# A third store behind k's blocks, sums of x in other pairs, a first pair's weight behind its total

## The chip, the cores and the metric

The program runs on one core of a Trainium2 chip. The metric is the device time of one execution in microseconds (us); the time before is the median of three runs. A profiled execution of its own, with a span from its first to its last instruction, gives all durations below.

## The reference

Attention in which a query sees only the keys that fall into its hash bucket, and a two-layer network behind it:

```python
q_bits = (np.einsum('bhsd,dk->bhsk', q, proj) > 0)      # 6 bits of each query, k likewise
mask = q_bucket[:, :, :, None] == k_bucket[:, :, None, :]
scores = np.where(mask, scale * q @ k.T, -1e9)
x = softmax(scores) @ v            # (4, 8, 768, 64) -> (3072, 512)
h = x @ w_in                       # (512, 2048)
g = np.maximum(h, 0.0) + alpha * np.minimum(h, 0.0)
out = g @ w_out                    # (2048, 512)
```

There are 4 batches of 8 heads, 768 positions each, 64 numbers a head. The weights come as 64-bit floats and are rounded to 32-bit ones on the chip.

## The kernel before

The work has two parts. The first runs over 16 pairs of heads (`pi` from 0 to 15, four pairs a batch). The second runs over blocks of the two matrix products, each built from seven smaller products in place of eight, which is why sums and differences of quarters of x, w_in, g and w_out are formed; `sum_x` forms those of x, and `sums_due` holds those of w_in.

In a pair, TensorE makes twelve cells of scores (L786: two matmuls on the hash bits `qb` and `kb`, four on q and k), ScalarE takes the exponential of each into `pt` (L789), then TensorE makes the next pair's hash bits (L738), multiplies the probabilities with v (`av`, L819, 96 matmuls), and sums columns for the softmax (`sm`, L832, in `totals`), which needs VectorE's total `accd` of the six blocks of probabilities. VectorE forms that total in five additions of 1.75 us each (`add_first` L797, `add_third` L805, `add_last` L801 and L802, `add_total` L808). The scores use a ring of three PSUM buffers (`two_banks`), which `sm`, the hash products and the turned alpha (L561) share.

The next pair's iteration opens with `divide` of the pair before: VectorE turns the sums (L846) and takes reciprocals, GpSimd copies four small blocks (L855, L856), VectorE spreads them (L858) and scales (L864). The result goes to DRAM as `x_s` (L865), from which `load_x` (L879) gets the quarters of batch 0 later. Between these lies `weight_begin`: the turn of the next pair's k blocks (L718), work on a weight piece, in four of the pairs a `sum_x` (L889), and the pair's first addition.

Each pair also rounds two weight pieces: `weight_abs` (ScalarE L606, L610, or VectorE L608), `weight_clamp` (L616), `weight_parts` (L622), `weight_sum` (L647, L650). Four pieces of w_in make a group; four sums on GpSimd (L669) follow, at most two a pair, and then the group's store: four DMAs (L674) into `w_in_s`, 448 KB each. There are four groups, so four stores. `load_w` (L895) later reads 896 KB of `w_in_s` for one block of the second part.

The order of work is the order of the program for everything inside `do(...)`; `pinned(when, ins)` does so only if `when` is true. DMAs outside are placed by the scheduler. One queue, SP's, issues almost all loads and stores, one after the other: at the end of pair `pi` those of v for pair `pi + 2` (L491), stores that are due, `load_w`, `load_x`, and the q and k blocks of pair `pi + 3` (L517, four DMAs each). Those blocks are turned by VectorE (L718) at the end of pair `pi + 1` (q) and at the start of pair `pi + 2` (k). The hash bits are moved into `qb` and `kb` by small DMAs on ScalarE's and GpSimd's queues (L747). GpSimd also issues the loads of the weight pieces (L592).

Of the kernel before, what the change touches and what calls it, by code (L numbers as in the profile page):

```python
# [407 lines left out]
def fast_path(  # L408
# [12 lines left out]
    nc = tc.nc  # L421
# [21 lines left out]
    do = tc.keep_in_program_order  # L443
# [66 lines left out]
    def load_blocks(pi, name):  # L510
        b, hp = pairs[pi]
        src = {"q": q, "k": k}[name]
        nat[name, pi] = t = pool.tile([P, NC * 4, 32], F32, name=f"{name}n{pi}", tag=f"{name}n", bufs=3)
        for s in range(2):
            for h in range(2):
                a = D * s + 32 * h
                nc.sync.dma_start(  # L517
                    t[a : a + 32].rearrange("i (c u) d -> i c u d", u=4),
                    src[b, 2 * hp + s, :, 32 * h : 32 * h + 32].rearrange("(u i c) d -> i c u d", u=4, c=NC),
                )  # L520

    nil = []

# [64 lines left out]
    def load_weight(i, queue=nc.gpsimd):  # L588
        if i < NW:
            i = order[i]  # L590
            raw[i] = pool.tile([P, 512], moe_w_in.dtype, name=f"raw{i}", tag="raw", bufs=3)
            queue.dma_start(raw[i], piece(i))  # L592
# [8 lines left out]
    def weight_abs(i, engine=None):  # L601
        i = order[i]
        lo, hi = halves(i)
        wx[i] = pool.tile([P, 512], F32, name=f"wx{i}", tag="wx")
        wr[i] = pool.tile([P, 512], I32, name=f"wr{i}", tag="wr")
        do(ACT.activation(wr[i], lo, AF.Copy, scale=2.0 ** -29))  # L606
        if engine is DVE:
            do(DVE.tensor_scalar(wx[i].bitcast(U32), hi, 0x7FFFFFFF, None, op0=ALU.bitwise_and))  # L608
            return
        do(ACT.activation(wx[i], hi.bitcast(F32), AF.Abs))  # L610

    def weight_clamp(i):
        if i < NW:
            i = order[i]
            x = wx[i]
            do(DVE.tensor_scalar(x, x, HI_MIN, None, op0=ALU.max, op1=ALU.max, accum_out=wmax[:, i : i + 1]))  # L616

    def weight_parts(i):
        i = order[i]
        x = wx[i].bitcast(U32)  # L620
        turned = i < HW and i % 4 == 3
        do(DVE.tensor_scalar(  # L622
            x, x, 3, 0x40000000 if turned else 0xC0000000, op0=ALU.logical_shift_left, op1=ALU.bitwise_xor,
        ))

    def weight_sum(i):


        i = order[i]
        lo, hi = halves(i)  # L630
        x = wx[i]
        if i < HW:
            n, m = divmod(i, 4)
            if m == 0:
                wst[n] = pool.tile([P, NM, 4, P], F32, name=f"wsi{n}", tag="wsi")
            slot = (0, 5, 1, 2)[m]
            dst = wst[n][:, slot].rearrange("p i f -> p (i f)")
        else:
            n, m = divmod(i - HW, 2)
            if m == 0:  # L640
                wst[HW + n] = pool.tile([P, 4, DM // 2], F32, name=f"wso{n}", tag="wso")
            w = wst[HW + n]
            dst = w[:, 0:4:3] if m == 0 else w[:, 1:3]
        x, r = x.bitcast(I32), wr[i]
        if i >= HW:
            hi, x, r = (t.rearrange("p (a f) -> p a f", a=2) for t in (hi, x, r))
        do(DVE.scalar_tensor_tensor(  # L647
            x.bitcast(U32), hi, 0x80000000, x.bitcast(U32), op0=ALU.bitwise_and, op1=ALU.bitwise_xor,
        ))
        do(DVE.tensor_tensor(dst.bitcast(I32), x, r, op=ALU.add))  # L650
        return (dst if i < HW else dst[:, 0])[:, :1]
# [3 lines left out]
    def weight_group(i):  # L655

        i = order[i]
        if i >= HW:
            n, m = divmod(i - HW, 2)
            if m == 1:  # L660
                nc.sync.dma_start(w_out_r[:, :, n].rearrange("m p d -> p m d"), wst[HW + n])
            return
        n, m = divmod(i, 4)
        if m < 3:
            return
        w = wst[n]

        def one(to, a, op, c):
            do(POOL.tensor_tensor(w[:, to], w[:, a], w[:, c], op=op))  # L669

        def store():
            c, kk = divmod(n, 2)
            for ii in range(4):
                do(nc.sync.dma_start(w_in_s[4 * c + ii][:, :, kk], w[:, :, ii]))  # L674


        for x in ((3, 5, 2), (5, 0, 5), (4, 3, 0), (6, 1, 4)):
            sums_due.append((one, (x[0], x[1], ALU.subtract, x[2])))
        sums_due.append((stores_due.append, (store,)))
# [5 lines left out]
    def weight_sums(count, after=None):  # L685

        if sums_due and after is not None:
            do(POOL.tensor_copy(late_sum, after))
        while sums_due and (count or sums_due[0][0].__name__ != "one"):
            fn, x = sums_due.pop(0)  # L690
            count -= fn.__name__ == "one"
            fn(*x)
            if now_stored and stores_due:
                stores_due.pop()()
# [21 lines left out]
    def turn_blocks(pi, name):  # L716
        tr[name, pi] = pool.tile([P, S], F32, name=f"{name}T{pi}", tag=f"{name}T")
        do(DVE.transpose(tr[name, pi], nat[name, pi].rearrange("p w d -> p (w d)")))  # L718
# [88 lines left out]
    def add_total(pi):  # L807
        do(DVE.tensor_tensor(accd[pi], accd[pi], accp[pi], op=ALU.add))  # L808
# [61 lines left out]
    def pinned(when, ins):  # L870

        if when:
            do(ins)
# [10 lines left out]
    def sum_x(b, n, engine):  # L884

        to, a, c = ((3, 5, 0), (5, 2, 5), (4, 2, 3), (6, 4, 1))[n]
        if to != 5:
            x_m[b, to] = mid.tile([P, 2, CW], F32, name=f"x{b}_{to}", tag=f"x{to}", bufs=1)
        do(engine.tensor_tensor(x_m[b, to], x_m[b, a], x_m[b, c], op=ALU.subtract))  # L889

    def load_w(n):

        if n < B * NI:
            w_m[n] = mid.tile([P, NM, 2, P], F32, name=f"wi{n}", tag="wi", bufs=3)
            pinned(n < 3, nc.sync.dma_start(w_m[n], w_in_s[n % NI]))  # L895
# [297 lines left out]

    for pi in range(NPAIR):
        i = 2 * pi
        if pi == 14:
            now_stored.append(pi)

        def weight_begin():
            if pi == 1:  # L1200
                turn_blocks(2, "q")
            if pi + 1 < NPAIR:
                turn_blocks(pi + 1, "k")
            weight_clamp(i)
            weight_parts(i)
            if pi in (8, 10, 12, 14):
                sum_x(0, (8, 10, 12, 14).index(pi), DVE)
            add_first(pi)

        if pi == 1:  # L1210
            scores(1, CELLS[:3])
            weight_abs(3)
            scores(1, CELLS[3:])
            divide(0, weight_begin)
        elif pi:
            scores(pi, CELLS)
            divide(pi - 1, weight_begin)
        else:
            rest = [c for c in CELLS if c not in ahead]
            scores(pi, rest[:4])  # L1220
            weight_abs(0, DVE)
            scores(pi, rest[4:])
            add_first(pi)
            weight_clamp(0)
            weight_parts(0)
        weight_sum(i)
        weight_group(i)
        load_weight(i + 3)
        if pi == 0:
            weight_abs(1, DVE)  # L1230
        weight_clamp(i + 1)
        add_third(pi)
        add_last(pi)
        add_total(pi)
        weight_parts(i + 1)
        weight_sums(1, weight_sum(i + 1))
        weight_group(i + 1)
        load_weight(i + 4)
        if pi + 1 < NPAIR:
            hash_bits(pi + 1)  # L1240
            do(ACT.activation(tr["q", pi + 1], tr["q", pi + 1], AF.Copy, scale=DOWN))  # L1241
        if 0 < pi < NPAIR - 2:
            turn_blocks(pi + 2, "q")
        attend(pi)
        if pi + 1 == NPAIR:
            now = ff1(0, 0)
            now.step(1)
        totals(pi)
        if pi + 1 == NPAIR:
            now.step(5)  # L1250
            divide(pi)
        else:
            weight_abs(i + 2)
        if pi + 2 < NPAIR:
            load(pi + 2, "v")
        while stores_due and pi < 14:
            stores_due.pop(0)()
        if pi in (9, 11, 15):
            load_w((9, 11, 15).index(pi))
        if pi in (4, 5, 7, 8):  # L1260
            load_x(0, {4: 0, 5: 3, 7: 2, 8: 1}[pi])
        if pi == 1:
            setup_alpha()
        for name in "qk":
            magnitude(pi, name)
            if pi + 3 < NPAIR:
                load(pi + 3, name)
        if 0 < pi < NPAIR - 1:
            weight_abs(i + 3)

# [96 lines left out]
```

## Time and profile before

| what | value |
|---|---|
| median of three runs | 874.98 us (873.43 to 875.38) |
| profiled execution, its own time | 872.97 us |
| its span | 871.19 us |
| TensorE's mean granted clock | 0.997 |
| bytes moved by DMA | 135.36 MB, 155 GB/s on average |

| `sm` (L832) of pair | starts at, us | since the one before |
|---|---|---|
| 0 | 28.65 | |
| 1 | 48.15 | 19.50 |
| 2 | 67.59 | 19.44 |
| 3 | 86.57 | 18.98 |
| 8 | 181.47 | 18.98 |
| 9 | 200.50 | 19.03 |
| 12 | 257.44 | 18.98 |
| 13 | 278.13 | 20.69 |
| 14 | 297.78 | 19.65 |
| 15 | 318.03 | 20.25 |

The second table is read from the timeline of TensorE: as every pair has one such group of matmuls, at the same place in its work, the distance between two of them is the time of a pair. A line of a timeline has the start and the duration in us, the engine, the line of the program, the operation, the tile that it writes and those that it reads, and in brackets how long the engine was idle before it and what ended that. SPq is SP's queue; a row there is the issue of DMAs, not their transfer. `x3` means three instructions in a row.

### The profile page before, as it was taken

To read this page: it belongs to the slowest core of one execution; us is meant where nothing else is said; L and a number is where in the kernel's file an instruction comes from. 1 tells how busy PE (TensorE), PEld (TensorE's weight loads), DVE (VectorE), ACT (ScalarE), POOL (GpSimd) and SP (SyncE) were. 2 spreads that over 40 slices of the span, in tenths; PEclk is the share of its full clock that TensorE was granted. 3 is DMA by queue.
4 is the path that set the end of the run, shared out by engine and by line. 5 is a ranking of instruction groups with operands and counts; after the bars stand their busy time and mean duration, and the time that the engine had idled before them with its cause. 6 is when DMAs were issued, how large, how long until landed. Compare 5 with 4: busy or idle time off the path is not lost.

```text
span 871.2 us, 14629 instructions
## 1 busy us (share of the span) xinstructions
PE 859.3 (99%) x5458; PEld 574.3 (66%) x5458; DVE 733.7 (84%) x1188; ACT 375.2 (43%) x682; POOL 121.5 (14%) x249
## 2 busy tenths in 40 slices
PE   9999999999999999999999999999999999999996
PEld 4444444444444445569995559996558997557996
DVE  6999999999998987899897669897659898568886
ACT  6687888878777733331113331112332112232111
POOL 1322423434424410210000000000000000000001
PEclk9999999999999999999999999999999999999998
DMA  8855779789696446785334344433425334420242
GB/s 196 178 146 130 176 180 248 176 215 232 130 265 158 148 131 237 262 288 221 118 116 121 133 134 156 123 145 90 175 86 170 138 109 127 151 84 1 97 163 61
DMA packets 171105, 135.36 MB, mean 155 GB/s; under 512 B 126240, under 2 KB 155088, under 8 KB 167440
## 3 DMA queue, kind: packets, MB, share of 16 engines
q1 hardware_dynamic: 158528, 108.44, 43.6%
q0 software_dynamic: 9488, 24.56, 9.2%
q10 hardware_dynamic: 3008, 1.33, 0.6%
q8 instruction: 45, 0.74, 0.4%
q14 instruction: 36, 0.29, 0.1%
HBM read 104.87 MB, written 28.31 MB: 153 GB/s over the span
## 4 chain that ended last, share of the span: by engine, by line


## 5 line engine op out<-in xcount | busy, mean ns | idle before, releaser
L786 PE MATMUL sc<-qT,kT 64*128 64x384 f32 x768 | 155.4, 482 | 0.0
L789 ACT ACTIVATE pt<-sc 128x768 f32<-128x768 f32 x192 | 151.8, 812 | 4.7 <-PE sc L786 4.5
L819 PE MATMUL av<-pt,vn 128*32 128x385 f32 (+1 forms) x1536 | 127.0, 485 | 0.0
L819 PEld LDWEIGHTS av<-pt,vn 128*32 128x32 f32 x1536 | 50.3, 109 | 73.8 <-issue 70.2
L786 PEld LDWEIGHTS sc<-qT,kT 64*128 64x128 f32 x768 | 68.9, 187 | 34.8 <-issue 34.0
L979 DVE TENSOR_TENSOR g<-g,g 128x384 f32<-128x384 f32 x128 | 68.4, 555 | 2.2
L1098 POOL DMA_DIRECT2D out_dram<-o x4 | 2.2, 555 | 472.8 <-DVE o L1091 472.8
L786 PE MATMUL sc<-qb,kb 64*128 64x384 bf16 x384 | 64.2, 324 | 1.5 <-DVE st L846 0.9
L975 DVE SCALAR_TENSOR_TENSOR g<-h,alpha 128x384 f32<-128x384 f32 x60 | 36.9, 614 | 25.2 <-ACT h L968 25.1
L1036 DVE TENSOR_TENSOR ws<-wl 128x512 f32<-128x512 f32 x56 | 38.5, 687 | 20.6 <-DMA wl<-w_out_s 18.8
L1044 DVE TENSOR_TENSOR gs<-g,gs 128x768 f32<-128x768 f32 x56 | 53.3, 952 | 1.0
L1044 DVE TENSOR_TENSOR gs<-g 128x768 f32<-128x768 f32 x56 | 53.3, 952 | 0.0
L786 PEld LDWEIGHTS <-kb 64*128 64x128 bf16 x384 | 21.3, 94 | 37.5 <-issue 13.7
L606 ACT ACTIVATE wr<-raw 128x512 int32<-128x512 uint32 x32 | 22.1, 691 | 33.4 <-DVE wso L650 17.8
L797 DVE TENSOR_TENSOR accp<-pt,pt 128x1536 f32<-128x1536 f32 x16 | 28.1, 1756 | 6.1 <-ACT pt L789 6.1
L747 POOL DMA_DIRECT2D qb<-hr x60 | 30.0, 507 | 21.3 <-ACT hr L742 21.3
L802 DVE TENSOR_TENSOR accd<-accd,pt 128x1536 f32<-128x1536 f32 x16 | 28.1, 1759 | 1.7
L808 DVE TENSOR_TENSOR accd<-accd,accp 128x1536 f32<-128x1536 f32 x16 | 28.1, 1758 | 0.6
L805 DVE TENSOR_TENSOR accp<-accp,pt 128x1536 f32<-128x1536 f32 x16 | 28.1, 1754 | 0.0
L801 DVE TENSOR_TENSOR accd<-pt,pt 128x1536 f32<-128x1536 f32 x16 | 28.0, 1752 | 0.0
L1241 ACT ACTIVATE qT<-qT 128x768 f32<-128x768 f32 x15 | 12.7, 845 | 26.7 <-DMA kb<-hr 16.2
L919 PE MATMUL f_0a<-x,wi 128*128 128x384 f32 x64 | 23.5, 490 | 0.0
(366 smaller groups left out, 1768.4 us busy)
## 6 DMA issues: line engine op xcount, KB each, us to landing
wi<-w_in_s SPq DMA_DIRECT2D x32, 896.0 KB
wl<-w_out_s SPq DMA_DIRECT2D x16, 1024.0 KB
wl<-w_out_r SPq DMA_DIRECT2D x12, 1024.0 KB
raw<-in_moe_w_in_dram POOLq DMA_DIRECT2D x15, 512.0 KB, 5.3
raw<-in_moe_w_out_dram POOLq DMA_DIRECT2D x14, 512.0 KB, 4.8
w_in_s<-wsi SPq DMA_DIRECT2D x16, 448.0 KB
qn<-in_q_dram SPq DMA_DIRECT2D x64, 96.0 KB
vn<-in_v_dram SPq DMA_DIRECT2D x16, 384.0 KB
```

Of the source, the lines that this page charges most:

```text
L747: queue.dma_start(bits[name, pi][D * s : D * s + 2 * NB, half * CW : (half + 1) * CW], raw[c : c + 2 * NB],)
L786: do(PE.matmul(sc[:, s, :CW], what["k", pi][r, ks], what["q", pi][r, qs], start=first, stop=not first,))
L789: do(ACT.activation(pts[kc][:, g, :, :CW], sc[:, :, :CW], AF.Exp, scale=SCALE / DOWN))
L797: do(DVE.tensor_tensor(accp[pi], p(0), p(1), op=ALU.add))
L802: do(DVE.tensor_tensor(accd[pi], accd[pi], p(5), op=ALU.add))
L805: do(DVE.tensor_tensor(accp[pi], accp[pi], p(2), op=ALU.add))
L808: do(DVE.tensor_tensor(accd[pi], accd[pi], accp[pi], op=ALU.add))
L819: do(PE.matmul(av[pi][D * s + t : D * s + t + 32, g, :w], nat["v", pi][:, s, kc * D + t : kc * D + t + 32], pts[kc][:, g, s, :w], start=(k ...
L975: do(DVE.scalar_tensor_tensor(new_g(b, m)[:, i], h, al, h, op0=ALU.mult, op1=ALU.max))
L979: do(DVE.tensor_tensor(new_g(b, to)[:, i], g_m[b, x][:, i], g_m[b, y][:, i], op=ALU.subtract))
L1036: do(DVE.tensor_tensor(t, w2[b, n, x], w2[b, n, y], op=op))
L1044: do(DVE.tensor_tensor(t, g2[b, n, x], g2[b, n, y], op=ALU.subtract))
```

## The change

Six things change in the order of the program; no operation is added or removed.

1. In pair 0, the second weight piece (L608, L616) follows the pair's total instead of standing ahead of `add_third`. Its `weight_sum` and the load of the next piece move further, into `divide` of pair 0 in the iteration of pair 1, ahead of the turn of q's blocks.
2. The third store of w_in's sums (group 2) is issued in pair 11 behind the loads of q and k, whose blocks for pair 14 are pinned in program order (k alone needs it). In the other pairs the loop that issues due stores is as it was.
3. The second `load_w` moves from pair 11 to pair 12.
4. The sums of x move from pairs 8, 10, 12, 14 to 6, 9, 12, 15.
5. The loads of x move from pairs 4, 5, 7, 8 to 3, 4, 6, 9.
6. The fourth store is no longer pinned, and `now_stored` is set from pair 12 on; on SP the store keeps its place.

```diff
-                nc.sync.dma_start(
+                pinned(name == "k" and pi == 14, nc.sync.dma_start(
                     t[a : a + 32].rearrange("i (c u) d -> i c u d", u=4),
...
-                do(nc.sync.dma_start(w_in_s[4 * c + ii][:, :, kk], w[:, :, ii]))
+                pinned(n < 3, nc.sync.dma_start(w_in_s[4 * c + ii][:, :, kk], w[:, :, ii]))
...
-        if pi == 14:
+        if pi == 12:
             now_stored.append(pi)
+
+        def weight_end(i):
+            weight_sums(1, weight_sum(i))
+            weight_group(i)
+            load_weight(i + 3)
 
         def weight_begin():
             if pi == 1:
+                weight_end(1)
                 turn_blocks(2, "q")
...
-            if pi in (8, 10, 12, 14):
-                sum_x(0, (8, 10, 12, 14).index(pi), DVE)
+            if pi in (6, 9, 12, 15):
+                sum_x(0, (6, 9, 12, 15).index(pi), DVE)
             add_first(pi)
...
-        if pi == 0:
-            weight_abs(1, DVE)
-        weight_clamp(i + 1)
+        if pi:
+            weight_clamp(i + 1)
         add_third(pi)
         add_last(pi)
         add_total(pi)
+        if pi == 0:
+            weight_abs(1, DVE)
+            weight_clamp(1)
         weight_parts(i + 1)
-        weight_sums(1, weight_sum(i + 1))
-        weight_group(i + 1)
-        load_weight(i + 4)
+        if pi:
+            weight_end(i + 1)
...
-        while stores_due and pi < 14:
+        while stores_due and pi < 10:
             stores_due.pop(0)()
-        if pi in (9, 11, 15):
-            load_w((9, 11, 15).index(pi))
-        if pi in (4, 5, 7, 8):
-            load_x(0, {4: 0, 5: 3, 7: 2, 8: 1}[pi])
+        if pi in (9, 12, 15):
+            load_w((9, 12, 15).index(pi))
+        if pi in (3, 4, 6, 9):
+            load_x(0, {3: 0, 4: 3, 6: 2, 9: 1}[pi])
...
+        if stores_due and pi == 11:
+            stores_due.pop()()
```

More of the change, by code (lines that the diff above doesn't have):

```diff
@@ L516, in load_blocks @@
                 a = D * s + 32 * h
-                nc.sync.dma_start(
+                pinned(name == "k" and pi == 14, nc.sync.dma_start(
                     t[a : a + 32].rearrange("i (c u) d -> i c u d", u=4),
                     src[b, 2 * hp + s, :, 32 * h : 32 * h + 32].rearrange("(u i c) d -> i c u d", u=4, c=NC),
-                )
+                ))
     nil = []
```

## The prediction

> **What bounds the kernel now.** First the page's busy times, then its row of 40 slices:
>
> ```profile
> PE 859.3 (99%) x5458; PEld 574.3 (66%) x5458; DVE 733.7 (84%) x1188; ACT 375.2 (43%) x682; POOL 121.5 (14%) x249
> ...
> PE   9999999999999999999999999999999999999996
> ```
>
> TensorE is busy for 859.3 of 871.2 us and its clock is full, so only its 11.9 us of gaps can be won or widened. The table of windows of 20 us says where they lie:
>
> ```profile
> 20.00:40.00 20.00, 18.70 (x180) 8.95 (x176) 18.96 (x27) 14.39 (x24) 5.36 (x13) 1.00 0.95 163
> ...
> 240.00:260.00 20.00, 19.93 (x192) 9.67 (x189) 18.80 (x26) 15.71 (x25) 5.83 (x13) 1.00 1.00 270
> 260.00:280.00 20.00, 19.05 (x186) 8.91 (x183) 17.51 (x25) 13.81 (x21) 6.37 (x15) 1.00 0.67 162
> 280.00:300.00 20.00, 19.53 (x190) 9.49 (x188) 19.27 (x27) 15.28 (x24) 9.95 (x17) 1.00 0.39 123
> ```
>
> (Columns: window, length, PE, PEld, DVE, ACT, POOL, clock, DMA share, GB/s.) From 320 us on every window but the last has PE at 19.99 or 20.00; the tail is not touched. So I read the attention part by its clock: the sums matmuls `sm` (L832), one group a pair. On the PE timeline they start at 28.65, 48.15, 67.59, 86.57, 105.55 and so on, 18.98 apart, until 257.44; then 278.13, 297.78, 318.03. Periods above 18.98 are lost time: 0.52 (pair 1), 0.46 (pair 2), 1.71 (13), 0.67 (14); pair 15 has other work in it (20.25). What ended the gaps, from the timelines of PE, weight loads, VectorE and the SP queue:
>
> ```profile
> 28.65 0.85 PE L832 MATMUL sm<-accd,ones 128*32 128x384 f32 x8 [0.97 <-DVE accd L808]
> ...
> 258.20 0.09 PEld L786 LDWEIGHTS <-kb 64*128 64x128 bf16 x1 [0.62 <-DMA kb<-hr]
> ...
> 260.81 0.34 PE L786 MATMUL sc<-qb,kb 64*128 64x384 bf16 x2 [0.41 <-DVE st L846]
> ...
> 278.13 0.85 PE L832 MATMUL sm<-accd,ones 128*32 128x384 f32 x8 [0.54 <-DVE accd L808]
> ```
>
> ```profile
> 259.31 0.98 DVE L718 STREAM_TRANSPOSE qT<-qn 128x768 f32<-128x768 f32 x1 [0.82 <-DMA qn<-in_q_dram]
> ...
> 263.44 0.98 DVE L718 STREAM_TRANSPOSE kT<-kn 128x768 f32<-128x768 f32 x1 [2.11 <-DMA kn<-in_k_dram]
> ```
>
> ```profile
> 242.29 5.81 SPq L674 DMA_DIRECT2D w_in_s<-wsi  x4
> 248.15 0.70 SPq L895 DMA_DIRECT2D wi<-w_in_s  x1
> 248.89 1.86 SPq L517 DMA_DIRECT2D qn<-in_q_dram  x2
> 250.85 8.29 SPq L517 DMA_DIRECT2D kn<-in_k_dram  x4
> ```
>
> The third store and a `wi` load stand ahead of pair 14's q and k blocks on SP. The blocks come late, VectorE stands still 0.82 + 2.11 us (it has about 0.7 us to spare a pair: its usual wait at L797), and TensorE waits for it in pairs 13 and 14.
>
> **What the Trainium skill says.** "DMA: Bandwidth & Descriptors", Queues, rings and completion order: each DMA engine consumes a queue's descriptors in ring order. The trace agrees: q's blocks, issued by 250.75, were waited for until 259.31, behind 1.79 MB of store and 0.90 MB of `wi` (2.69 MB at the 341 to 365 GB/s of 244 to 252 us is an estimated 7.6 us). Same page, Issuing engines are not separate DMA queues: DMAs of SP, ScalarE and GpSimd share the same 16 engines. Agrees: the hash bits `qb`, on GpSimd's queue, took 6.6 us to land between 245 and 265 against a median of 4.1. "SBUF — State Buffer", SBUF: two separate sides: a VectorE operation with two SBUF inputs and a GpSimd operation that reads SBUF exclude each other. Agrees: GpSimd's copies at L855, 0.19 us alone, took 1.63 at 284.62 beside the sum of x and the add at L797.
>
> **Part 1, pair 0's second weight behind the total.** L608 and L616 stood between 20.36 and 21.42 ahead of L805: 1.06 us. Without them the total L808 ends at 28.50 - 1.06 = 27.44, and `sm` starts at 27.59 (0.15 after it, as before); TensorE is ready at 27.49 (av at 19.74, plus the 7.75 from av to sm of a pair without a wait). So 1.06 us at this place. But the work isn't gone: VectorE does the same operations before qT of pair 2, which stays at 31.37, and reaches L797 at 34.24. Before, it waited there 0.52 us for ScalarE (34.76), so VectorE gains only 0.52. Does that hold TensorE? In pair 1, the total ends at 47.39 - 0.52 = 46.87 and `sm` could start at 47.09: no wait. In pair 2 the second cell starts at 50.18, right after VectorE's copy of alpha (L562, 49.99), which stands behind qT: that moves by 0.52 only. So of 1.06 us, 0.52 stays. Bounds: 0 if ScalarE also has to wait (its L606 of weight 3 would now come at about 31.7, the buffer of weight 1 comes free at about 31.5), 1.06 if the copy does not bind. GpSimd's load of weight 4 goes from 29.86 to about 31.5, is needed at 43.6 and lands in some 5.3 us: nothing.
>
> **Part 2, the third store behind k's blocks, the second `wi` load from pair 11 to 12.** All of its DMAs count: four stores (5.81 us of SP) and one load (0.70) leave the place ahead of q and k. Then q is issued by 244.2 and k by about 249.1 (four k issues cost 4.1 to 6.3 us in pairs 2 to 10). With only v ahead they land by about 252; needed at 258.5 and 260.5. Both waits go. What TensorE gets back: in pair 13 the third cell's late start, 0.64 us (1.45 between cells in place of 0.81) and the late sum, 0.72 (9.14 from hash to sums in place of 8.42); in pair 14, where VectorE is still behind, 0.67 (the third cell again); in pair 15 0.30 (the fourth cell comes 1.11 after the third, since ScalarE's L606 waits for a late L650). Sum 2.33. The first cell's 0.34 in pair 13 was a wait for hash bits. They are sent at 250 to 254, and the store now runs beside them, at 249 to 255, where before `wi` and k's blocks did; I leave that 0.34 standing. Bounds: 0.34 more gain, or a microsecond of loss if the bits land at 7.6 us. What is queued behind the store on SP is x_s, at about 255 in place of 259.24: earlier. `wi` lands in pair 12 ahead of pair 15's blocks, 0.7 us for SP; k's were issued by 269.9 and are needed at about 281: hidden.
>
> **Part 3, sums and loads of x moved.** One sum is 0.95 us. In pairs 6, 9 and 12 it meets VectorE's wait of 0.7 at L797; the 0.25 left over is covered by the 1.3 us between the end of a total and `sm` (85.28 to 86.57), which is why pairs 8 and 10 lost at most 0.05 so far. In pair 15 a wait of 1.09 at L797 and no blocks to turn. Without GpSimd's sums beside it the copies at L855 no longer stretch, and the waits at L858 (2.2 us in 5) shrink; TensorE waited for none. I take 0 (0.05 either way). The x loads: x_1 now stands beside `wi` in pair 9, 1.28 MB, an estimated 3.7 us at 345 GB/s ahead of half of q and all of k, which were issued by 211.8 and are needed at about 220: 4 us to spare. Pair 8 loses its x load beside a store, which only helps.
>
> **Sum.** 0.52 + 2.33 + 0 = 2.85, say 2.9 us. The profiled execution took 872.97 (span 871.19 and 1.8 around it): 870.1. The median of the timed runs, 874.98, is 2.0 above it; I keep that offset: 872.1. Its cause isn't visible; if it is the same late blocks, they cost more there and the gain grows.
>
> **Rivals.**
> A, a wait takes the place (17%): hash bits or q and k of a neighbouring pair keep most of the stall, and 0.5 to 1.5 us remain of the gain: about 874. For it: DMA share is 1.07 to 1.15 from 244 to 256 and the bytes there fall by a third only. Against: blocks of all other pairs come in time.
> B, larger (10%): the timed runs' 2 us are late blocks too, and go: 874.98 - 5 = 870.0. For it: DMA arrival is what can vary from run to run. Against: nothing shows it.
> C, slower (11%): pair 13's bits behind the store. Each microsecond by which they land later than 6.6 us holds TensorE at its first cell for one. The gain is eaten at 6.6 + 2.9 = 9.5 us; at 12 us the time is 874.98 - 2.9 + 5.4 = 877.5. Against: the longest landing seen is 6.9, with the engines as full.
> That the edits don't take effect is excluded for order: on SP the new program has k's four blocks, then the store, then x_s.
>
> **How the numbers follow.** The forecast has 62%, 872.1, own range 870.8 to 873.1. A change under 0.2% (1.75 us) can't be told from none here. Faster: all of B, nearly all of the forecast: 0.71. Same: A and the forecast's weak end: 0.18. Slower: 0.11. The range reaches to B's and A's times: 869.8 to 874.8.
>
> **What would show it.** Right: `sm` of pairs 12 to 14 at 18.98 us from each other; no DMA wait at qT and kT; sums of pair 0 at about 27.6 with some 0.5 us left by pair 3. Wrong: long waits for `kb<-hr` at about 258; a new wait for q or k near 220; `sm` of pair 3 not earlier than 86.57.

## The result and the profile after

| | before | after |
|---|---|---|
| median of 14 runs each, side by side | 873.12 us (872.03 to 875.60) | 869.57 us (868.60 to 873.30) |
| profiled execution | 872.97 us | 869.49 us |
| its span | 871.19 us | 867.7 us |
| `sm` of pair 15 starts at | 318.03 us | 313.75 us |
| from there to the end of the span | 553.16 us | 553.95 us |

The ratio after / before is 0.9962 with an interval of 0.9949 to 0.9974: 3.3 us faster (2.3 to 4.5), where 2.9 were forecast. The forecast of 872.1 is 2.5 above the median. Most of that is its base: three runs had given 874.98 for the kernel before, fourteen give 873.12, so the 2.0 us that the forecast added on top of the profiled execution were not there. The median lies below the forecast's own range of 870.8 to 873.1; put on the forecast's base, the measured ratio gives 0.9962 x 874.98 = 871.7. One execution of the kernel before, in the batch of e1 to e4 below, took 2374.82 us and is left out of the ratios.

The page of the changed kernel, busy time and the 40 slices:

```profile
PE 857.9 (99%) x5458; PEld 572.7 (66%) x5458; DVE 732.7 (84%) x1188; ACT 377.5 (44%) x682; POOL 115.2 (13%) x249
...
PE   9999999999999999999999999999999999999996
```

The gaps of TensorE fell from 11.9 to 9.8 us (867.7 - 857.9) and its busy time by another 1.4. Busy time is not all work: from 200 to 320 us the kernel before lost 2.7 us against the changed one (table below), and its windows show 1.63 of that as gaps. Part of the rest stands as busy time: waiting for `kb` made the first matmuls of pair 13's first cell 0.74 long, against 0.34 now. So the page alone gives 3.5 us and no place. The windows (columns as before) give the place:

```profile
20.00:40.00 20.00, 19.68 (x196) 9.84 (x192) 19.48 (x28) 15.18 (x24) 5.65 (x13) 1.00 1.00 170
240.00:260.00 20.00, 20.00 (x194) 9.50 (x192) 19.58 (x29) 16.14 (x24) 5.84 (x12) 1.00 1.13 275
260.00:280.00 20.00, 20.00 (x196) 9.56 (x194) 18.33 (x26) 16.23 (x25) 8.74 (x20) 1.00 0.79 201
280.00:300.00 20.00, 20.00 (x194) 9.44 (x192) 18.53 (x24) 16.23 (x24) 6.66 (x13) 1.00 0.42 137
```

From 240 us on, TensorE now has no gap in the attention part. Its timeline, one `sm` a pair and what lies between:

```profile
27.06 0.83 PE L832 MATMUL sm<-accd,ones 128*32 128x384 f32 x8
...
48.64 0.34 PE L786 MATMUL sc<-qb,kb 64*128 64x384 bf16 x2 [0.16 <-DVE alpha L562]
...
85.03 0.83 PE L832 MATMUL sm<-accd,ones 128*32 128x384 f32 x8
...
255.85 0.83 PE L832 MATMUL sm<-accd,ones 128*32 128x384 f32 x8
...
257.43 0.33 PE L786 MATMUL sc<-qb,kb 64*128 64x384 bf16 x2
...
258.24 0.33 PE L786 MATMUL sc<-qb,kb 64*128 64x384 bf16 x2
...
274.83 0.83 PE L832 MATMUL sm<-accd,ones 128*32 128x384 f32 x8
...
293.81 0.83 PE L832 MATMUL sm<-accd,ones 128*32 128x384 f32 x8
...
313.75 0.85 PE L832 MATMUL sm<-accd,ones 128*32 128x384 f32 x8
...
440.09 1.57 PE L919 MATMUL z_4a<-g,wl 128*128 128x192 f32 x8 [0.76 <-DMA wl<-w_out_r]
```

Pairs 13 and 14 take 18.98 (274.83 - 255.85, 293.81 - 274.83), pair 15 takes 19.94. The third cell of pair 13 comes 0.81 after the second; before, it was 1.45. The first sum has no wait left, and pair 2's second cell still waits for alpha. The last line is new: the second part waits once for a block of w_out. Of the 4.28 us by which `sm` of pair 15 is earlier, 0.79 are given back behind it; 3.49 remain, the difference of the profiled executions.

The queue of SP (start, duration of the issues), and VectorE where it stood still before:

```profile
242.68 3.44 SPq L517 DMA_DIRECT2D kn<-in_k_dram  x4
246.22 4.65 SPq L674 DMA_DIRECT2D w_in_s<-wsi  x4
250.97 3.29 SPq L865 DMA_DIRECT2D x_s<-x  x1
...
257.24 0.94 SPq L895 DMA_DIRECT2D wi<-w_in_s  x1
```

```profile
256.37 0.97 DVE L718 STREAM_TRANSPOSE qT<-qn 128x768 f32<-128x768 f32 x1
...
258.29 0.97 DVE L718 STREAM_TRANSPOSE kT<-kn 128x768 f32<-128x768 f32 x1
...
260.91 1.76 DVE L797 TENSOR_TENSOR accp<-pt,pt 128x1536 f32<-128x1536 f32 x1 [0.61 <-ACT pt L789]
```

k's blocks are issued by 246.12, before by 259.14. Both turns run without a wait, and VectorE waits for ScalarE again at its first addition (0.61), as in an undisturbed pair.

The gain by place, from the `sm` starts of both traces:

| where | won, us | forecast |
|---|---|---|
| before `av` of pair 0 (19.74 to 19.31) | 0.43 | not forecast |
| `av` of pair 0 to `sm` of pair 3 (66.83 to 65.72) | 1.11 | 0.52 |
| pair 9 (19.03 to 18.98) | 0.05 | 0, within 0.05 |
| pair 13 (20.69 to 18.98) | 1.71 | 1.36 |
| pair 14 (19.65 to 18.98) | 0.67 | 0.67 |
| pair 15 (20.25 to 19.94) | 0.31 | 0.30 |
| behind pair 15 | -0.79 | 0 |
| sum | 3.49 | 2.85 |

The sum fits better than its terms deserve: two of them, 0.43 and -0.79, come from no edit. Three questions remain: which of the two moves on SP makes the late blocks arrive in time; whether pair 15's 0.31 has to do with these blocks at all; and what the edit in pair 0 is worth, since its gain stands beside an earlier start that no edit accounts for.

### The profile page after: what moved, and what is told of

It reads as the page before. It is cut to its first block, busy times and chain, and to the rows that moved or that the text cites. A ratio compares the mean times of both kernels' runs of the same rounds, so it can differ in the third digit from the quotient of the medians.

```text
span 867.7 us, 14629 instructions
## 1 busy us (share of the span) xinstructions
PE 857.9 (99%) x5458; PEld 572.7 (66%) x5458; DVE 732.7 (84%) x1188; ACT 377.5 (44%) x682; POOL 115.2 (13%) x249
## 4 chain that ended last, share of the span: by engine, by line
## 5 line engine op out<-in xcount | busy, mean ns | idle before, releaser
L789 ACT ACTIVATE pt<-sc 128x768 f32<-128x768 f32 x192 | 153.9, 812 | 3.1 <-PE sc L786 2.8
L797 DVE TENSOR_TENSOR accp<-pt,pt 128x1536 f32<-128x1536 f32 x16 | 28.1, 1756 | 7.2 <-ACT pt L789 7.2
L802 DVE TENSOR_TENSOR accd<-accd,pt 128x1536 f32<-128x1536 f32 x16 | 28.1, 1759 | 1.7
```

What stands on the lines that cost most here:

```text
L789: do(ACT.activation(pts[kc][:, g, :, :CW], sc[:, :, :CW], AF.Exp, scale=SCALE / DOWN))
L797: do(DVE.tensor_tensor(accp[pi], p(0), p(1), op=ALU.add))
L802: do(DVE.tensor_tensor(accd[pi], accd[pi], p(5), op=ALU.add))
```

## The experiments

### Pair 0's second weight: alone, and taken out

e1 is the kernel before with this edit alone. Its main part:

```diff
...
-        if pi == 0:
-            weight_abs(1, DVE)
-        weight_clamp(i + 1)
+        if pi:
+            weight_clamp(i + 1)
         add_third(pi)
         add_last(pi)
         add_total(pi)
+        if pi == 0:
+            weight_abs(1, DVE)
+            weight_clamp(1)
...
```

> The kernel before with pair 0's edit alone. Theory (the weight behind the total gives 0.5 to 1.1 us, how much depends on when weight 0 and pair 1's k blocks arrive at the start): from av of pair 0 to sm of pair 0 7.75 us in place of 8.91; from av of pair 0 to sm of pair 3 shorter by 0.5 to 1.1 than the 66.83 of before; pairs 13 and 14 keep their 20.69 and 19.65 within 0.5; time 0.5 to 1.2 us below before. Rival (the gain at pair 0 is eaten by the copy of alpha in pair 2): sm of pair 3 no earlier against av of pair 0 than before, pair 2's period longer by what pair 0 won.

Measured: 872.88 against 873.38 us, ratio 0.9994 (0.9985 to 1.0003). The first sum comes 7.75 us after `av`, with no wait; pairs 13 to 15 take 20.84, 19.66 and 20.26, as long as in the kernel before to within 0.15. The interval includes 1, so a gain in time is not shown by these runs.

e9 is the changed kernel with this edit undone (the lines above in reverse, and `weight_end(1)` back at the end of pair 0).

> The changed kernel with pair 0's edit undone. Theory (sm of pair 0 is then bound by VectorE, which starts when weight 0 has arrived, and in the changed kernel by TensorE): sm of pair 0 8.2 to 9.1 us behind av's start in place of 7.75, sm of pair 3 at 85.9 to 86.6 in place of 85.0 to 85.8; pairs 13 and 14 at 18.98, pair 15 at 19.94; time 0.3 to 1.1 us above the changed kernel, ratio to before 0.9965 to 0.998. Rival (pair 0's edit is worth nothing once the rest is in): sm of pair 3 as in the changed kernel, ratio 0.996.

Measured: 870.42 us, ratio 0.9969 (0.9958 to 0.9980). `sm` of pair 3 comes 66.16 after `av`; with the edit 65.72. The intervals of e9 and of the changed kernel overlap, and the two did not run side by side; their ratios differ by 0.0007, 0.6 us, which these runs do not tell from nothing.

Why the profiles showed 1.11 and not 0.52 is seen at VectorE's start. Its timeline before:

```profile
15.71 0.43 DVE L608 TENSOR_SCALAR wx<-raw 128x512 uint32<-128x512 uint32 x1 [0.78 <-DMA raw<-in_moe_w_out_dram]
16.05 1.75 DVE L797 TENSOR_TENSOR accp<-pt,pt 128x1536 f32<-128x1536 f32 x1
```

and after:

```profile
14.72 0.43 DVE L608 TENSOR_SCALAR wx<-raw 128x512 uint32<-128x512 uint32 x1 [0.53 <-DMA raw<-in_moe_w_out_dram]
15.06 1.75 DVE L797 TENSOR_TENSOR accp<-pt,pt 128x1536 f32<-128x1536 f32 x1
...
26.36 0.44 DVE L608 TENSOR_SCALAR wx<-raw 128x512 uint32<-128x512 uint32 x1
...
33.23 1.75 DVE L797 TENSOR_TENSOR accp<-pt,pt 128x1536 f32<-128x1536 f32 x1
```

The first addition cannot start before the first weight has arrived from DRAM, and this start moves by a microsecond from run to run. In the old order, `sm` of pair 3 stands 70.5 us behind this addition in six runs: 70.52 in the kernel before, 70.49 in e2, 70.53 in e3, 70.51 in e4 and e6, 70.53 in e9. That is a chain of VectorE, which does not care when `av` starts. Only in e5, where the addition started 5.07 us ahead of `av` (3.69 in the kernel before), does TensorE set the time: 65.65 after `av`.

In the new order VectorE's chain is shorter. From its first addition to that of pair 1 it takes 18.71 us in the kernel before and 18.10 in e7 (further below), which up to there is the changed kernel, and whose lead over `av`, 3.75, is about as small. In the kernel before (its first addition at 16.05 is shown above),

```profile
34.76 1.76 DVE L797 TENSOR_TENSOR accp<-pt,pt 128x1536 f32<-128x1536 f32 x1 [0.52 <-ACT pt L789]
```

and in e7:

```profile
16.07 1.75 DVE L797 TENSOR_TENSOR accp<-pt,pt 128x1536 f32<-128x1536 f32 x1
...
34.17 1.75 DVE L797 TENSOR_TENSOR accp<-pt,pt 128x1536 f32<-128x1536 f32 x1
```

In the profile of after, `sm` of pair 3 stands 69.97 behind the first addition (85.03 - 15.06), 0.55 less than the 70.52 of the old order. The addition itself came 0.99 earlier (15.06 in place of 16.05), and no edit stands ahead of it. Together these are the 1.54 by which `sm` of pair 3 is earlier. Of the 0.99, the table above has 0.43 ahead of `av` and the other 0.56 inside the 1.11, so the edit's share of the 1.11 is 0.55.

With VectorE further ahead the edit wins less, because TensorE then sets the time: 65.72 and 65.87 after `av` in the changed kernel and in e1, at leads of 4.25 and 4.55. Against this 65.72 it wins 0.44 at e9's lead of 4.37 and nothing at e5's. At the lead of 3.69 the new order was not seen without other edits; e7, at 3.75, has 65.75, but alpha's copy is off VectorE there.

### The two moves on SP, together and one at a time

e2 is the kernel before with the third store behind k and the load of `wi` in pair 12:

```diff
-                nc.sync.dma_start(
+                pinned(name == "k" and pi == 14, nc.sync.dma_start(
...
-        if pi == 14:
+        if pi == 12:
             now_stored.append(pi)
...
-        while stores_due and pi < 14:
+        while stores_due and pi < 10:
             stores_due.pop(0)()
-        if pi in (9, 11, 15):
-            load_w((9, 11, 15).index(pi))
+        if pi in (9, 12, 15):
+            load_w((9, 12, 15).index(pi))
...
+        if stores_due and pi == 11:
+            stores_due.pop()()
```

> The kernel before with the store behind k's blocks and the second wi load in pair 12, nothing else. Theory (these two carry pairs 13 to 15): periods of pairs 13 and 14 18.98, of pair 15 19.9 to 20.0, no wait of qT or kT for a DMA; time 2.3 to 2.9 us below before. Rival (the sums of x, which keep GpSimd's copies from being stretched, are needed too): pair 14, which still has a sum of x beside GpSimd's sums here, keeps 0.3 us or more of its loss.

Measured: 870.40 us, ratio 0.9967 (0.9955 to 0.9979), so 2.9 of the 3.3 us. Pairs 13 and 14 take 19.04 and 18.98. Pair 15 still takes 20.21: not what the prediction says.

e3 keeps the load of `wi` in pair 11; all else is as in e2.

> Like the run before it, but the second wi load stays in pair 11, ahead of q's last two blocks and k's. Theory (store's 1.79 MB is the main cause, wi's 0.90 MB alone fits, since in pair 9 a wi load stands there too): no wait for blocks, pairs 13 and 14 at 18.98. Rival (any large transfer ahead of them is too much): kT of pair 14 waits 0.5 us or more and pair 13 is over 19.2.

e4 moves only that load, and the store stays ahead of q and k:

```diff
-        if pi in (9, 11, 15):
-            load_w((9, 11, 15).index(pi))
+        if pi in (9, 12, 15):
+            load_w((9, 12, 15).index(pi))
```

> The kernel before with the second wi load in pair 12 alone; the store stays ahead of the blocks, as it does in pairs 5 and 8. Theory: 5.8 us of issue remain ahead of them, so the blocks come 2 to 3 us sooner than before: about the 2.1 us that kT waited, so pair 13 loses 0 to 0.5 us in place of 1.71. Rival (the store alone is enough to make them late): pair 13 keeps 1 us or more.

Measured, one run each: e3 870.38 us with pairs 13 and 14 at 19.03 and 18.98; e4 869.97 us with 19.19 and 18.98. Neither has a wait at the turns of q and k. SP's queue in e3:

```profile
242.32 0.62 SPq L895 DMA_DIRECT2D wi<-w_in_s  x1
242.98 1.78 SPq L517 DMA_DIRECT2D qn<-in_q_dram  x2
244.86 5.41 SPq L517 DMA_DIRECT2D kn<-in_k_dram  x4
250.37 6.24 SPq L674 DMA_DIRECT2D w_in_s<-wsi  x4
```

and in e4, with VectorE's turn of k below it:

```profile
241.77 5.92 SPq L674 DMA_DIRECT2D w_in_s<-wsi  x4
247.73 2.09 SPq L517 DMA_DIRECT2D qn<-in_q_dram  x2
249.93 6.50 SPq L517 DMA_DIRECT2D kn<-in_k_dram  x4
```

```profile
259.76 0.97 DVE L718 STREAM_TRANSPOSE kT<-kn 128x768 f32<-128x768 f32 x1
```

In e4 k's last issue ends at 256.43 and its block has landed at 259.76 at the latest, so within 3.3 us. In the kernel before, the last issue ended at 259.14 and the turn could start at 263.44, after 4.3. So 0.90 MB ahead of these blocks does no harm, 1.79 MB does none either, and 2.69 MB is too much: each move alone wins nearly all of the stall, and the second one adds nothing that one execution of each shows. Whether the bytes count or the time that SP takes to issue is not separated: k's four issues took 8.29 us before, 6.50 in e4, 5.41 in e3 and 3.44 in the changed kernel. The rival, that the store ahead alone makes them late, falls with e4. The 0.15 to 0.2 of pair 13 that e4 still loses is the first cell, 0.97 to the next one in place of 0.81: there the bits `kb`, as far as GpSimd sends them, take 5.6 to 5.9 us to land, in the kernel before 5.8 to 5.9, but 5.3 to 5.6 in the changed kernel, 5.2 to 5.4 in e2 and 4.5 to 4.8 in e3, all three without this wait. This is the wait of 0.34 that the prediction left standing; it goes when the store is behind k.

### Pair 15: late blocks, or the sum of x?

e5 is the kernel before with the moved sums and loads of x alone; e6 is e2 with only the last sum moved, from pair 14 to 15:

```diff
-            if pi in (8, 10, 12, 14):
-                sum_x(0, (8, 10, 12, 14).index(pi), DVE)
+            if pi in (8, 10, 12, 15):
+                sum_x(0, (8, 10, 12, 15).index(pi), DVE)
```

> The kernel before with the moved sums and loads of x alone. First theory (x's moves are worth 0 to 0.05 us): pair 15 keeps 20.14 to 20.26, pair 13 about 20.7, pair 14 0.3 or more over 18.98. Second theory, formed after the two runs with the store or wi moved alone, whose pair 15 stayed at 20.25 and 20.14 with pair 14 clean (pair 15's late cell comes from the sum of x in pair 14, beside GpSimd's sums): pair 15 at 19.9 to 20.0, pair 9 at 18.98 in place of 19.03, though the blocks are still late; pair 13 still over 20; time 0.3 to 0.9 us below before.

> The store behind k's blocks, wi in pair 12, and of x's moves only the last sum from pair 14 to pair 15; no loads of x move. Second theory (pair 14's sum delays VectorE's L650 in pair 15 and so ScalarE's exponentials): pair 15 19.9 to 20.0, pair 9 still 19.03, pair 13 19.03. First theory (pair 15's 0.3 came from the late blocks; here it should be gone, but it was not): pair 15 20.2.

Measured, one run each: e5 872.01 us (873.57 before), with pair 15 at 19.94 and pair 9 at 18.98, while pairs 13 and 14 keep 20.64 and 19.65. e6 870.87 us, with pair 15 at 19.94 and pair 9 at 19.03. So pair 15's 0.3 follows the last sum and not the blocks, and pair 9's 0.05 goes with the rest of that edit. How a sum in pair 14 costs time in pair 15 is seen on VectorE in e2, where the sum stands in pair 14 (`sm` of pair 13 at 276.38),

```profile
281.11 0.95 DVE L889 TENSOR_TENSOR x<-x,x 128x768 f32<-128x768 f32 x1
281.98 1.75 DVE L797 TENSOR_TENSOR accp<-pt,pt 128x1536 f32<-128x1536 f32 x1
284.05 0.98 DVE L858 STREAM_TRANSPOSE dn<-rr 128x768 f32<-128x768 f32 x1 [0.32 <-POOL rr L856]
```

and in e6, where it does not (`sm` of pair 13 at 275.86):

```profile
280.92 1.76 DVE L797 TENSOR_TENSOR accp<-pt,pt 128x1536 f32<-128x1536 f32 x1 [0.23 <-ACT pt L789]
283.00 0.98 DVE L858 STREAM_TRANSPOSE dn<-rr 128x768 f32<-128x768 f32 x1 [0.32 <-POOL rr L856]
```

The first addition comes 5.60 after `sm` in e2 and 5.06 in e6: the sum's 0.95 eats VectorE's whole wait for ScalarE and 0.54 more. Both then wait 0.32 for GpSimd at L858, which the changed kernel does not. At the last addition of that pair but one (L802) VectorE is 15.07 behind `sm` in e2, 14.55 in e6 and 14.13 in the changed kernel. 0.42 of lateness costs TensorE nothing and 0.94 costs 0.27. e4, which also keeps the sum in pair 14, lies between: there VectorE is 14.81 behind, 0.68 late, and pair 15 takes 20.14, 0.20 more. So the slack at this place lies between 0.42 and 0.68. In e2 the weight's last step (L650) then ends late and ScalarE begins the exponentials of pair 15 2.62 after `sm`; in e6 2.09, in the changed kernel 1.80.

GpSimd's copy that L858 waits for, in e2:

```profile
282.15 1.63 POOL L855 COPY rr<-rr 32x12 f32<-32x12 f32 x1
```

It takes 0.19 in the changed kernel and 1.73 in e6, where it also falls under that addition. It starts beside the addition at 281.98, an operation with two inputs in SBUF, and ends with it. This agrees with what the prediction cites from the Trainium skill, "SBUF — State Buffer", SBUF: two separate sides. In the changed kernel the sum of GpSimd ahead of the copies ends earlier, at 278.83, 4.00 after `sm` in place of 4.43 in e2, so all four copies have begun before the addition does; why that sum ends earlier was not traced.

### What is still lost in pairs 1 and 2

After the change these two take 19.51 and 19.48, 1.03 more than two undisturbed pairs. The trace names the copy of alpha in pair 2, and a wait of 0.3 for ScalarE in pair 1, which works on weight 3 between two cells. e7 is the changed kernel with alpha's copy on ScalarE, behind the squares of q and k; e8 has in addition the absolute value of weight 3 on VectorE, ahead of its clamp in pair 1:

```diff
-        do(DVE.tensor_copy(alpha, ps))
+        do(ACT.copy(alpha, ps))
...
```

> The changed kernel, with the copy of alpha (L562) on ScalarE behind the squares of q and k in place of VectorE behind the turn of q. Theory (TensorE's second cell in pair 2 waits for the place of that copy in VectorE's order, which is why part of pair 0's gain can be lost there): pair 2 at 19.1 to 19.2 (0.16 for alpha's matmul stays) in place of 19.48, time 0.3 us below the changed kernel. Rival (the cell waits for VectorE's turn of the sums L846, in the same ring of PSUM buffers): pair 2 stays at 19.4 to 19.5.

> Like the run before it, and in pair 1 the absolute value of weight 3 on VectorE ahead of its clamp, so that ScalarE does L606 alone between the third and the fourth exponential. Theory (pair 1's 0.5 over 18.98 is ScalarE's 1.25 us there): ScalarE 0.6 less, pair 1 at 19.0 to 19.1 in place of 19.51; pair 2 at 19.1 to 19.3; time 0.5 to 0.8 us below the changed kernel, about 0.9955 of before. Rival (VectorE, which has no wait left in pair 1, becomes the bound): a wait of sm in pair 1 for the total, or pair 2 longer by what pair 1 won.

Measured: e7 868.92 us in one execution, e8 869.26, ratio 0.9961 (0.9949 to 0.9973): no gain over the changed kernel. (e7's lower time lies behind pair 15, where it takes 552.8 us; its `sm` of that pair comes 0.59 later than in the changed kernel.) TensorE in e7,

```profile
49.99 0.34 PE L786 MATMUL sc<-qb,kb 64*128 64x384 bf16 x2 [0.17 <-DVE st L846]
```

and in e8, where lines are shifted by two:

```profile
47.02 0.85 PE L834 MATMUL sm<-accd,ones 128*32 128x384 f32 x8 [0.61 <-DVE accd L810]
...
50.07 0.34 PE L788 MATMUL sc<-qb,kb 64*128 64x384 bf16 x2 [0.32 <-DVE st L848]
```

In e7 pair 2 stays at 19.49: the same stall, one cell later, now put down to the turn of the sums. In e8 VectorE has 0.4 us more to do in pair 1 and its total is late. The name that a wait carries was only the last of VectorE's operations ahead of it; VectorE is behind in these pairs.

So e10 takes work from it: alpha's copy is on ScalarE as in e7, the absolute value of weight 1 goes to ScalarE too, and ScalarE's work on weight 3 stands one cell later.

```diff
...
-            scores(1, CELLS[:3])
+            scores(1, CELLS[:4])
             weight_abs(3)
-            scores(1, CELLS[3:])
+            scores(1, CELLS[4:])
...
         if pi == 0:
-            weight_abs(1, DVE)
+            weight_abs(1)
             weight_clamp(1)
...
```

e11 is e10 with the absolute value of weight 3 on VectorE, as in e8.

> The changed kernel with less for VectorE in pairs 0 to 2: weight 1's absolute value on ScalarE (L610 in place of L608), weight 3's on ScalarE after four cells in place of three, so that VectorE's first addition in pair 1 waits less, and alpha's copy on ScalarE. Theory (VectorE's chain holds pair 2's third cell): VectorE 0.4 us earlier, pair 2 at 19.1 to 19.2 in place of 19.48, pair 1 still about 19.5; 0.3 us below the changed kernel. Rival (ScalarE becomes the bound of pairs 0 and 1): pair 1 at 19.6 or more, or sm of pair 0 later than 7.8 behind av.

> Like the run before it, and weight 3's absolute value on VectorE ahead of its clamp in pair 1, ScalarE with L606 alone after four cells. Theory (both engines then have room): no wait of sm for the total in pair 1 above 0.2 us, pair 1 at 19.0 to 19.3, pair 2 at 19.1 to 19.4, sum of both below 38.7 in place of 38.99. Rival (VectorE stays the bound, as in the run that had only this step): sum of both 39.0 or more.

Measured: e10 868.45 us (868.22 to 869.66), ratio 0.9951 (0.9938 to 0.9964); pairs 1 and 2 take 19.62 and 19.14. e11 869.08 in one execution, with 19.31 and 19.65. Both pairs together: 38.99 in the changed kernel, 38.76 in e10, 38.96 in e11, 39.44 in e8. Pair 2's stall shrinks when VectorE has less to do and comes back when it has more, which is what VectorE as the bound would give. But only 0.23 of the 1.03 come back, since TensorE in e10 still loses 0.32 to ScalarE in pair 1, and e11 moves that loss from pair 1 to pair 2 and decides nothing:

```profile
34.49 0.34 PE L786 MATMUL sc<-qb,kb 64*128 64x384 bf16 x2 [0.32 <-ACT pt L789]
```

e10 is the fastest of all by its median. Against the kernel before that is shown; against the changed kernel it is not: the intervals overlap, and the two did not run side by side.

## Why the prediction was right, and where its terms were off

**The stall of pairs 13 and 14** was right in place, cause and size. Of the 2.38 us won there, 2.03 were in the sum. The rest is the 0.34 of the hash bits of pair 13, which the prediction kept as a bound and left standing because the store would run beside them: it does, and `kb` lands in 5.3 to 5.6 us in place of 5.8 to 5.9. e3 and e4, one execution each, put this on the store's place and not on `wi`; why a store beside the bits is milder than one ahead of them is open.

**Part 2 needed one move, not two.** The prediction took both away at once and gave no share to each. In e3 and e4, one execution each, either alone sufficed.

**Pair 15's 0.30 is the step that failed.** The prediction saw the late L650 and ScalarE behind it, and counted it among the effects of the late blocks; the same 0.30 stays in e2, where the blocks come in time, and goes in e5, where they do not. It is the sum of x in pair 14. Part 3 was therefore not worth 0 but 0.36 us (0.31 in pair 15, 0.05 in pair 9), and part 2 0.30 less than in the sum. The prediction had both halves in hand, a stretched copy at 284.62 beside that very sum and a wait at L858, and stopped at "TensorE waited for none". But TensorE waits a pair later, for ScalarE, which waits for VectorE; no wait in the trace points back to the sum.

**Pair 0.** Mechanism and size were right: no wait at the first sum, VectorE loses its wait at L797 and keeps 0.61 of the 1.06 (0.52 in the prediction), and the copy of alpha still holds pair 2. At the start that the profile of after had, the edit is worth 0.55. It is no constant, though, for it depends on how far VectorE is ahead of `av`: 0.44 in e9, nothing in e5. By the timed runs of e1 it is 0.5 (-0.3 to 1.3).

**Luck.** Of the 3.49 us between the two profiles, 0.99 are VectorE's earlier start, which no edit brought, and 0.79 were lost again behind pair 15. Neither was forecast, and they nearly cancel. What the edits won by these traces is 3.29 (0.55, 0.05, 1.71, 0.67 and 0.31), against the 2.85 of the sum.

**What came back.** The 0.79 us are lost to the wait at 440.09. The load that it waits for is issued 119.11 us after `sm` of pair 15 in both kernels (432.86 and 437.14), and needed 6.5 us later; in the profile of before 1 MB arrived within that, in the profile of after it took 0.76 more. The changed kernel does nothing different there. Over all thirteen profiled executions this part takes 552.7 to 554.2 us, and the three longest have each a late block of w_out. In e1 (554.0) it is an earlier one: VectorE waits for it, and TensorE later for VectorE.

```profile
386.94 0.69 DVE L1036 TENSOR_TENSOR ws<-wl 128x512 f32<-128x512 f32 x1 [1.44 <-DMA wl<-w_out_r]
```

```profile
402.37 1.57 PE L919 MATMUL z_2c<-gs,ws 128*128 128x192 f32 x8 [0.78 <-DVE m L1065]
```

e6 (554.2) has the same two waits, of 1.67 and 0.78. The other ten take 552.7 to 553.2. An earlier issue of these loads was not tried, and whether they are what spreads the timed runs, which left no trace, is open.

**The rivals.** A, a wait takes the place: no wait for q, k or the bits is left. C, bits behind the store: they land earlier, not later. B, a larger gain because the timed runs had more late blocks: its time of 870.0 came near, but its reason was not there, as the kernel before in more runs has a median of 873.12, close to its profile.

## What to carry to other kernels

A small operation on an engine that follows behind can cost nothing where it stands and something a stage later: compare how far that engine is behind a fixed group in each stage, with and without the operation, before pricing it at nothing because no wait names it. In a queue that several transfers share, ask how much may stand ahead of the urgent one; here either of two was harmless without the other, so the cheaper of two moves would have done. A gain near the start of a kernel depends on when the first data arrive, so measure the distance from that arrival and not from the start, and do not count an earlier arrival as a gain of the edit.

## What the runs showed of the hardware

- VectorE's first addition, which waits for data from DRAM, starts between 15.06 and 16.10 us in thirteen runs, with no edit ahead of it that explains this. Mostly the first weight comes last (a wait of 0.78 in the kernel before), in e10 k's blocks (1.66). The old order's chain behind the addition holds to 0.04 us in six of seven runs.
- A load of 1 MB that was in time with 6.5 us ahead of its use came 0.76 us late in another execution of the same code.
- A copy of 32 x 12 numbers on GpSimd, 0.19 us alone, takes 1.63 to 1.73 when it falls under an addition of VectorE with two inputs in SBUF. A shift of 0.4 us decides whether it does.
- Four loads of 96 KB each took SP 3.44 us to issue in the changed kernel, 5.41 in e3 with 0.90 MB ahead of them in the queue, 6.50 in e4 with 1.79 MB, and 8.29 in the kernel before with 2.69 MB, one execution each.
